# One attention visit for the second batch, casts on the DMA queue, and one more chunk of split products in the first tile of a fused attention and feed-forward kernel

## The chip, the core and the metric

The kernel runs on one core of a Trainium2 chip. The metric is the device time of one execution in microseconds (us). The profile is of one such execution and covers the five engines (PE for matrix products, ACT, DVE and POOL for elementwise work, SP for issuing transfers) and the core's 16 DMA engines.

## The reference

Linear attention over 8 batches (8 heads, 576 positions, head size 64), normalised per head, then a feed-forward layer over 4608 tokens of 512 features with 2048 hidden ones and a rational function between its two products:

```python
kv = np.einsum('bhsd,bhse->bhde', k, v)
out = np.einsum('bhsd,bhde->bhse', q, kv)
rms = np.sqrt(np.mean(out * out, axis=-1, keepdims=True) + 1e-06)
x = out / rms * g_norm            # to (tokens, 512)
h = x @ w_in
P = a[0] + a[1] * h + a[2] * h2 + a[3] * h3
Q = 1.0 + np.abs(b[0]) * np.abs(h) + np.abs(b[1]) * h2
return (P / (Q + 1e-06)) @ w_out
```

w_in and w_out come as 8-byte floats and are made into 4-byte ones on the chip.

## The kernel before

**Tiles and slots.** The tokens are cut into 9 tiles of 512: tile t holds the first 512 positions of batch t, and the ninth holds the last 64 positions of all batches. The hidden features are cut into 16 chunks of 128. One pair (tile, chunk) is a slot, and the loop at L784 writes the order of the instructions by hand (manual schedule): in slot i it issues the elementwise steps of h of chunk i (`ew_a` to `ew_d`, on ACT and DVE), the second product of slot i-2 (`gemm2`), the attention steps for the next tile that lists assign to the slot, the weight steps due in it, and the first product of slot i+1 (`gemm1`). Every engine works its own list in that order, so an instruction that waits holds all that stands behind it on its engine.

**Two kinds of products.** A "split" product takes both operands as a rounded high part and a low rest (type fp32r) and sums three matmuls (L531 to L533 for h, L599 to L601 for the output). An unsplit one is a single fp32 matmul, which the profile shows as two records (L527, L590). In tile 0, h of chunks 0 to `EARLY`-1 = 7 and all second products are unsplit.

**The front.** Before the loop, the k'v and the attention of batch 0 are done in a stage of their own. Its sums of squares (`first_ms`, L692), the reciprocal root (`first_newton`) and its spreading over 128 rows (`first_rb`, L708) work on blocks of `BW` = 64 columns, `NBLK` = 4 for each half tile.

**Attention of batch 1** is spread over tile 0 (`attention0`, L505). Each of four head pairs has a visit of its own: `att_kv1` (20 matmuls of 64 columns, L351, then two ACT copies into kvf, L270) in slots 1, 3, 5 and 7, and `att_o` (one fp32 matmul with q, L430, then a square and a copy on ACT, L438 and L439) in slots 2, 4, 6 and 8. All pairs share one PSUM buffer ("at") and one SBUF buffer for q ("qr"), so `att_o` fetches the next pair's q (`fetch_next_q`) only after its own matmul. It also fetches the next pair's k and v, and after the last pair the first of batch 2.

**Weights.** A unit is two chunks of w_in ("wi") or w_out ("wo"), 1 MiB as it comes. `schedule` (L141) holds for each unit the slot of its fetch (-1: before the loop), of its conversion (`signed` and `lowbits` on ACT, or `lowbits` on DVE for units in `ON_VECTOR`; `conv_b1`, `conv_add` on DVE) and of its split, and the rooms for its raw words, its fp32 form and its high and low parts.

**Split by transfer.** `split_w` casts the high part on ACT (L244). In the next slot POOL writes the negated high part (L250), and a POOL transfer adds the fp32 original to it in place (L251). `split_x0` does the same with x of tile 0, two head pairs at a time, its high part cast on ACT (L258) in slots 1 and 3.

**Queues.** All loads are issued by SP in program order, on one DMA queue (q1); transfers that cast or accumulate are issued by POOL (q0).

Of the kernel before, what the change touches and what calls it, by code (L numbers as in the profile page):

```python
# [23 lines left out]
def linear_attention_then_rational_ffn(  # L24
# [17 lines left out]
    P = 128  # L42
# [20 lines left out]
    NC = 7  # L63
    HW = TW // 2
    MAIN = 8 * P
    NBLK = 4
    BW = HW // NBLK
    kv0 = [wpool.tile([P, 2, MAIN], F32, tag=g, name=f"first_{g}") for g in ("g4", "g5")]
    qa0 = wpool.tile([P, NPAIR * HW + NC], F32, tag="g6", name="first_qa")
# [65 lines left out]
    def f32(t):  # L135
# [3 lines left out]


    schedule = {  # L141
# [16 lines left out]
    }  # L158
    units = list(schedule)

# [8 lines left out]
    for c in range(4, NF, 2):  # L169
        made[schedule["wi", c][1] + 1].append(("wi", c, None))  # L170

    EARLY = 8
    ON_VECTOR = (("wi", 6),)

    def unsplit(t, c):
        return t == 0
# [77 lines left out]
    def split_x0(g):  # L254
        pool, tag = ((xpool, "xA"), (wpool, "e"))[g]
        xt = pool.tile([P, 2, 2, TW], F32R, tag=tag, name=f"x_0_{g}")
        of = x0[:, 2 * g:2 * g + 2]
        ACT.copy(xt[:, :, 0], of)  # L258
        x.setdefault(0, []).extend((xt[:, p, 0], xt[:, p, 1]) for p in range(2))
        lows.append((xt[:, :, 1], xt[:, :, 0], of))  # L260

# [4 lines left out]
    def split_kv(t, pairs, ps):  # L266
        n = pairs.stop - pairs.start
        made = [ps[js, 0:n * D].rearrange("p (n d) -> p n d", n=n) for js in heads]
        for js, m in zip(heads, made):
            ACT.copy(kvf[js, pairs, js], m)  # L270
        if t == 1:
            return None
        for js, m in zip(heads, made):
            ACT.copy(kvh[js, pairs, js], m)

        def rest():
            for js in heads:
                DVE.tensor_tensor(kvl[js, pairs, js], kvf[js, pairs, js], f32(kvh[js, pairs, js]), ALU.subtract)
        return rest
# [28 lines left out]
    kvms, qrs, qs, sqs, rs, rbs, xf = {}, {}, {}, {}, {}, {}, {}  # L308

    def fetch_kv(t, p):  # L310
        tag, bufs = ("rb", 2) if p >= 2 and t > 1 else (f"kvm{p % 2}", 1)
        kvms[t, p] = work.tile([P, 2, 4, P], F32, tag=tag, name=f"kvm_{t}_{p}", bufs=bufs)
        nc.sync.dma_start(kvms[t, p], kv[t, p])

# [30 lines left out]
    def kv_products(t, ps, k, p):  # L345
        m = kvms.pop((t, p))
        ends = kvms[t][:, p // 2]
        for c in range(5):
            for js in heads:
                a, b = (m[:, 0, c], m[:, 1, c]) if c < 4 else (ends[:, 0], ends[:, 1 + p % 2])  # L350
                PE.matmul(ps[js, k * D:(k + 1) * D], a[:, js], b[:, js], start=(c == 0), stop=(c == 4))  # L351

    def att_kv1(t, p):
        ps = ps_at.tile([P, TW], F32, tag="at", name=f"kvp_{t}_{p}", bufs=1)
        kv_products(t, ps, 0, p)
        qs[t, p] = qrs.pop((t, p))
        split_kv(t, slice(p, p + 1), ps)

    def att_kv4(t, ps):
        if t >= NB:  # L360
            return None
# [2 lines left out]
        fetch_first_kv(t + 1)  # L364
        return lambda: split_kv(t, slice(0, NPAIR), ps)

    def att_kv_of_third(t, _):
        return att_kv4(t, ps_at.tile([P, TW], F32, tag="at", name=f"kvp_{t}", bufs=1))() if t == 2 else None

    x_rest = dram.tile([NPAIR, P, NB * R], F32, tag="x_rest", name="x_rest", bufs=1)  # L370

# [50 lines left out]
    def att_o(t, p):  # L422
        if t == LAST:
            sqs[t, p] = work.tile([P, TW], F32, tag="at", name=f"sq_{t}_{p}", bufs=4)
            ACT.activation(sqs[t, p], xf[t, p], AF.Square)
            return
        ps = ps_at.tile([P, TW], F32, tag="at", name=f"op_{t}_{p}", bufs=1)
        q = qs.pop((t, p))
        if t == 1:
            PE.matmul(ps, kvf[:, p], q, start=True, stop=True)  # L430
        else:
            qh, ql = q
            PE.matmul(ps, kvh[:, p], ql, start=True, stop=False)  # L433
            PE.matmul(ps, kvl[:, p], qh, start=False, stop=False)  # L434
            PE.matmul(ps, kvh[:, p], qh, start=False, stop=True)  # L435
        sq = work.tile([P, TW], F32, tag="at", name=f"sq_{t}_{p}", bufs=4)
        xf[t, p] = xpool.tile([P, TW], F32, tag=f"xf{p}", name=f"xf_{t}_{p}")
        ACT.activation(sq, ps, AF.Square)  # L438
        ACT.copy(xf[t, p], ps)  # L439
        sqs[t, p] = sq  # L440
        if t == 1:
            if p + 1 < NPAIR:
                fetch_kv(t, p + 1)
            else:
                fetch_first_kv(t + 1)
            fetch_next_q(t, p)

    def att_ms(t, _):
# [41 lines left out]
    attention = {s: [] for s in range(NF)}  # L490
    for p in range(NPAIR):
        if p == 0:
            attention[0].append((att_kv_of_third, 0))
        attention[2 * p].append((att_q, p))
        attention[2 * p + 1].append((att_o, p))
        attention[(11, 12, 13, 13)[p]].append((att_norm, p))
    attention[3].append((fetch_last_kv, 0))
    attention[8] += [(att_rest, 0), (att_ms, 0)]
    attention[9].append((att_rstd, 0))
    fillat = {att_norm: 1, att_kv_of_third: 1, att_rest: 1, att_q: 1, att_rstd: 2}  # L500
    attention[10] += [(att_rd, 0), (att_rb, 0), (att_rb, 1)]

    fillat0 = {}
    attention0 = {s: [] for s in range(NF)}
    for f, at in ((att_kv1, [1, 3, 5, 7]), (att_o, [2, 4, 6, 8]), (att_ms, [9]), (att_rstd, [9]), (att_rd, [10]), (att_rest_first, [10]), (fetch_last_kv, [11]), (att_rb, [11, 11]), (att_norm, [12, 12, 13, 13])):  # L505
        for p, k in enumerate(at):
            attention0[k].append((f, p))

# [224 lines left out]
            DVE.tensor_copy(x0[:, p, halves[0]], o0[p][0])  # L733
    for u in at_slot(0, -1)[:1]:
        fetch_w(u)
    fetch_kv(1, 0)
    fetch_ends(1)
    fetch_q(1, 0)
    for u in at_slot(0, -1)[1:]:
        fetch_w(u)  # L740
    ms0 = ps_at.tile([P, TW], F32, tag="ms", name="ms_0", bufs=1)
    first_ms(0)
    for p in range(NPAIR):
# [40 lines left out]
    for i, (t, c) in enumerate(slots[:-1]):  # L784
        q_made = ew_a(t, c, ph)
        for todo in lows:

            tc.add_manual_dep(low_by_transfer(*todo).ins, q_made.ins.name, beside, reason="negated beside h")
        lows.clear()
        if i:  # L790
            ew_d(*slots[i - 1])
        rest = {0: [], 1: [], 2: []}
        shifts = []
        convs = [lambda u=(k, n), j=j: conv_add(u, both if j is None else (one, two)[j]) for k, n, j in made.get(i, [])]

        ew_b(t, c, ph, convs[:1])
        if i == LAG:
            ph = gemm1(0, i + 1)
        if i >= LAG:
            gemm2(*slots[i - LAG])  # L800
            if slots[i - LAG][1] == NF - 1:
                evacuate(slots[i - LAG][0])
        for u in at_slot(2, i):
            split_w(u)
        if i in (1, 3):
            split_x0(i // 3)
        if i == 0:
            ph = h0[1]
        elif i in (1, 3):
            ph = gemm1(0, i + 1)  # L810
        if t + 1 < NTILE:
            for step, p in (attention0 if t == 0 else attention)[c]:
                todo_dve = step(t + 1, p)
                if todo_dve:
                    rest[fillat0.get(step, 2) if t == 0 else fillat[step]].append(todo_dve)
            for u in at_slot(0, i):
                fetch_w(u)
        for u in at_slot(1, i):
            signed(u)
            lowbits(u, both, "V" if u in ON_VECTOR else "S")  # L820
            shifts.append(u)
        rest[2] += convs[1:]
        if t == 0 and c == NF - 3:
            rest[2] += [split(1, p) for p in range(NPAIR // 2)]
        if t and c == NF - 2:
            ph = h_last
        elif 4 <= i < len(slots) - 2:
            ph = gemm1(*slots[i + 1])
            if 0 < t < NTILE - 1 and c == NF - 3:
                h_last = gemm1(t, NF - 1)  # L830
        if c == NF - 2 and t < NTILE - 1:
            xl = [split(t + 1, p) for p in range(NPAIR // 2 if t == 0 else 0, NPAIR)]
            if t == 0:
                rest[0] += xl
            for k in range(2 if t else 0):
                rest[k].append(xl[k])
                rest[2].append(xl[2 + k])
        if i == 0:
            rest[2].append(lambda: conv_add(u2, one))
        rest[2] += [lambda u=u: conv_b1(u, both) for u in shifts]  # L840
        ew_c(t, c, lambda k: [f() for f in rest[k]])
# [55 lines left out]
```

## Time and profile before

| | us |
|---|---|
| median of 3 runs | 879.95 (879.93 to 879.99) |
| profiled execution | 879.79 |
| its span, first to last instruction | 877.7 |
| PE busy | 870.7 (99%) |
| DVE busy | 757.7 (86%) |
| ACT busy | 687.5 (78%) |
| POOL busy | 73.3 (8%) |

The profiled execution takes 2.1 us beyond its span and lies 0.16 us under the median. In a timeline line the columns are: start, duration, engine, source line, operation, output and inputs, count and, in brackets, idle time of the engine before it with what ended it. Matmuls are pipelined, so that their records overlap; the distance from one start to the next is what a matmul costs. Tile 0 runs from about 24 us to 137 us.

### The profile page before, as it was taken

What the parts mean: (1) busy time and instruction counts of PE and PEld (TensorE: products, weight loads), DVE (VectorE), ACT (ScalarE), POOL (GpSimd) and SP (SyncE); (2) the same over time, 40 slices, a digit from 0 to 9 for tenths busy, and PEclk for the clock granted to TensorE, in tenths of its full rate; (3) what the DMA queues carried; (4) which work ended last, traced back from release to release, by engine and by line L of the source; (5) the groups of instructions that cost most, each with busy time, mean ns of one, the idle gap of its engine ahead of it and who ended that gap; (6) DMA issues with size and microseconds to landing.
All of it is one profiled execution on the core that took longest, in us unless ns stands there. A gap on an engine that the chain in (4) does not pass through costs nothing.

```text
span 877.7 us, 11994 instructions
## 1 busy us (share of the span) xinstructions
PE 870.7 (99%) x4468; PEld 683.9 (78%) x4468; DVE 757.7 (86%) x1185; ACT 687.5 (78%) x1142; POOL 73.3 (8%) x63
## 2 busy tenths in 40 slices
PE   9999999999999999999999999999999999999997
PEld 7545657888888888878888888888878887888886
DVE  4988998979987998879887998799879987998887
ACT  5999889877876788777877787768867786787665
POOL 2131435413000000000000000000000000000000
PEclk9999999999999999999999999999999999999999
DMA  9987638554122203040303111020102020201001
GB/s 364 406 262 226 145 73 216 138 127 97 60 73 90 50 6 115 30 122 1 119 19 104 31 61 72 25 50 17 69 12 50 13 84 1 49 1 49 1 0 49
DMA packets 32650, 76.27 MB, mean 87 GB/s; under 512 B 6032, under 2 KB 7568, under 8 KB 32592
## 3 DMA queue, kind: packets, MB, share of 16 engines
q1 hardware_dynamic: 29600, 65.81, 22.0%
q0 software_dynamic: 2848, 9.44, 5.9%
q8 instruction: 35, 0.57, 0.3%
q10 hardware_dynamic: 144, 0.26, 0.1%
q14 instruction: 23, 0.19, 0.1%
HBM read 55.45 MB, written 10.62 MB: 75 GB/s over the span
## 4 chain that ended last, share of the span: by engine, by line
PE 91%; DVE 5%; ACT 2%; issue 1%; DMA 1%; SPq 0%; ACTq 0%
PE h L531 14%; PE h L532 13%; PE h L533 13%; PE acc L599 12%; PE acc L601 12%; PE acc L600 12%; PE acc L590 5%; PE h L527 2%; PE kvp L351 2%; PE ms L451 1%; DMA first_g<-in_first_dram 1%; PE op L435 1%; PE op L433 1%; PE op L434 1%; DVE u L545 1%
## 5 line engine op out<-in xcount | busy, mean ns | idle before, releaser
L541 ACT ACTIVATE d<-h 128x512 f32<-128x512 f32 x143 | 85.6, 599 | 139.4 <-PE h L533 138.3
L543 DVE SCALAR_TENSOR_TENSOR q<-d,b1abs,q 128x512 f32<-128x512 f32 x143 | 107.2, 749 | 83.7 <-ACT q L542 83.5
L531 PE MATMUL h<-x,wihl 128*128 128x512 f32 (+1 forms) x420 | 166.2, 396 | 0.0
L532 PE MATMUL h<-x,wihl 128*128 128x512 f32 (+1 forms) x420 | 162.7, 387 | 0.0
L533 PE MATMUL h<-x,wihl 128*128 128x512 f32 (+1 forms) x420 | 162.6, 387 | 0.0
L599 PE MATMUL acc<-woh,gl 128*128 128x512 f32 x316 | 123.1, 389 | 0.1
L600 PE MATMUL acc<-wol,gh 128*128 128x512 f32 x316 | 122.9, 389 | 0.0
L601 PE MATMUL acc<-woh,gh 128*128 128x512 f32 x316 | 122.9, 389 | 0.0
L554 ACT ACTIVATE d<-q,bias 128x512 f32<-128x512 f32 x143 | 105.6, 738 | 13.9 <-DVE q L543 12.5
L544 ACT ACTIVATE u<-h,na 128x512 f32<-128x512 f32 x143 | 112.5, 787 | 0.0
L555 ACT ACTIVATE d<-d,bias 128x512 f32<-128x512 f32 x143 | 103.6, 725 | 4.7
L561 DVE SCALAR_TENSOR_TENSOR u<-u,na,d 128x512 f32<-128x512 f32 x143 | 106.7, 746 | 0.0
L551 DVE SCALAR_TENSOR_TENSOR u<-u,na,h 128x512 f32<-128x512 f32 x143 | 106.1, 742 | 0.6
L559 DVE SCALAR_TENSOR_TENSOR q<-q,d 128x512 f32<-128x512 f32 x143 | 98.4, 688 | 0.2 <-ACT d L555 0.2
L545 DVE TENSOR_TENSOR u<-u,h 128x512 f32<-128x512 f32 x143 | 98.0, 685 | 0.0
L542 ACT ACTIVATE q<-h,abg 128x512 f32<-128x512 f32 x143 | 97.9, 685 | 0.0
L531 PEld LDWEIGHTS h<-x,wihl 128*128 128x128 f32 x420 | 78.9, 188 | 24.0 <-issue 6.2
L532 PEld LDWEIGHTS h<-x,wihl 128*128 128x128 f32 x420 | 78.9, 188 | 17.0 <-issue 1.2
L533 PEld LDWEIGHTS h<-x,wihl 128*128 128x128 f32 x420 | 78.9, 188 | 16.2
L578 DVE TENSOR_TENSOR gl<-u,gh 128x512 fp32r<-128x512 f32 x127 | 90.8, 715 | 0.0
L567 DVE SCALAR_TENSOR_TENSOR u<-q,u 128x512 f32<-128x512 f32 x127 | 87.5, 689 | 2.5
L577 ACT CAST gh<-u 128x512 fp32r<-128x512 f32 x127 | 80.3, 632 | 3.5 <-DVE u L567 3.4
(170 smaller groups left out, 1403.0 us busy)
## 6 DMA issues: line engine op xcount, KB each, us to landing
kvm<-in_kv_dram SPq DMA_DIRECT2D x28, 512.0 KB
raw_wo<-in_w_out_dram SPq DMA_DIRECT2D x8, 1024.0 KB
out_dram<-ob SPq DMA_DIRECT2D x16, 512.0 KB
qr<-in_qT_dram SPq DMA_DIRECT2D x28, 256.0 KB
rb<-rd SPq DMA_DIRECT2D x28, 256.0 KB
raw_wi<-in_w_in_dram SPq DMA_DIRECT2D x6, 1024.0 KB
wihl<-wiw POOLq DMA_DIRECT2D x6, 512.0 KB, 4.7
kvt<-in_kv_rest_dram SPq DMA_DIRECT2D x7, 384.0 KB
```

The lines of the kernel that those rows point to most:

```text
L531: PE.matmul(ph, wh, xl, start=(kc == 0), stop=False)
L532: PE.matmul(ph, wl, xh, start=False, stop=False)
L533: PE.matmul(ph, wh, xh, start=False, stop=(kc == NPAIR - 1))
L543: q_made = DVE.scalar_tensor_tensor(q, d, b1abs, q, ALU.mult, ALU.add)
L544: ACT.activation(u, ph, AF.Identity, bias=na[:, 2:3], scale=na[:, 3:4])
L545: DVE.tensor_tensor(u, u, ph, ALU.mult)
L551: DVE.scalar_tensor_tensor(u, u, na[:, 1:2], ph, ALU.add, ALU.mult)
L554: ACT.activation(d, q, AF.Ln, bias=bias[:, 2:3], scale=QSC)
L561: DVE.scalar_tensor_tensor(u, u, na[:, 0:1], d, ALU.add, ALU.mult)
L599: PE.matmul(o, gl[:, ss], wh, start=(c == 0), stop=False)
L600: PE.matmul(o, gh[:, ss], wl, start=False, stop=False)
L601: PE.matmul(o, gh[:, ss], wh, start=False, stop=(c == NF - 1))
```

## The change

- `NBLK` goes from 4 to 2: the front's blocks have 128 columns.
- k'v of batch 1: the four `att_kv1` are replaced by one `att_kv` in slot 3 (80 matmuls, then two ACT copies for all pairs), `att_o` moves to slots 4, 5, 6 and 7, `att_rest_first` from slot 10 to slot 9. k and v of all four pairs and the first q are fetched before the loop, behind four weight units. The first k and v of batch 2 are fetched right behind the visit, in slot 3.
- x of tile 0: the high parts are cast by POOL transfers in slot 0, and the low parts follow one after the other, in slots 2 and 3 (before: 2 and 4).
- `EARLY` goes from 8 to 7: h of the eighth chunk is a split product. Unit ("wi", 6) is therefore split in slot 3 instead of 17, and its `lowbits` moves from DVE to ACT.
- The map of rooms is new; ("wi", 14) and ("wo", 10), ("wo", 12) and ("wo", 14) are fetched one or two slots later.

```diff
-    NBLK = 4
+    NBLK = 2
...
-        ("wi", 6): (-1, 1, 17, "g4", "f4", ("f10", "f12")),
+        ("wi", 6): (-1, 1, 3, "g4", "f4", "g4"),
...
-        ("wi", 14): (3, 8, 10, "g4", "f12", "g4"),
-        ("wo", 10): (4, 9, 23, "g5", "f13", ("f5", "f4")),
-        ("wo", 12): (6, 11, 25, "g7", "f14", ("f7", "f9")),
-        ("wo", 14): (8, 13, 27, "g1", "f15", ("f11", "f13")),
+        ("wi", 14): (4, 8, 10, "g5", "f12", "g5"),
+        ("wo", 10): (6, 9, 23, "g7", "f13", ("f3", "f5")),
+        ("wo", 12): (8, 11, 25, "g1", "f14", ("f7", "f9")),
+        ("wo", 14): (10, 13, 27, "g3", "f15", ("f11", "f13")),
...
-    EARLY = 8
-    ON_VECTOR = (("wi", 6),)
+    EARLY = 7
+    ON_VECTOR = ()
...
-        ACT.copy(xt[:, :, 0], of)
+        POOL.dma_start(xt[:, :, 0], of)
...
-        lows.append((xt[:, :, 1], xt[:, :, 0], of))
+        return xt[:, :, 1], xt[:, :, 0], of
...
-        tag, bufs = ("rb", 2) if p >= 2 and t > 1 else (f"kvm{p % 2}", 1)
+        tag, bufs = ("rb", 2) if p >= 2 else (f"kvm{p % 2}", 1)
...
-    def att_kv1(t, p):
-        ps = ps_at.tile([P, TW], F32, tag="at", name=f"kvp_{t}_{p}", bufs=1)
-        kv_products(t, ps, 0, p)
-        qs[t, p] = qrs.pop((t, p))
-        split_kv(t, slice(p, p + 1), ps)
...
-    def att_kv_of_third(t, _):
-        return att_kv4(t, ps_at.tile([P, TW], F32, tag="at", name=f"kvp_{t}", bufs=1))() if t == 2 else None
+    def att_kv(t, _):
+        if t <= 2:
+            return att_kv4(t, ps_at.tile([P, TW], F32, tag="at", name=f"kvp_{t}", bufs=1))()
...
         if t == 1:
-            if p + 1 < NPAIR:
-                fetch_kv(t, p + 1)
-            else:
-                fetch_first_kv(t + 1)
             fetch_next_q(t, p)
...
-    for f, at in ((att_kv1, [1, 3, 5, 7]), (att_o, [2, 4, 6, 8]), (att_ms, [9]), (att_rstd, [9]), (att_rd, [10]), (att_rest_first, [10]), (fetch_last_kv, [11]), (att_rb, [11, 11]), (att_norm, [12, 12, 13, 13])):
+    for f, at in ((att_kv, [3]), (att_o, [4, 5, 6, 7]), (att_rest_first, [9]), (att_ms, [9]), (att_rstd, [9]), (att_rd, [10]), (fetch_last_kv, [11]), (att_rb, [11, 11]), (att_norm, [12, 12, 13, 13])):
...
     for u in at_slot(0, -1)[:1]:
         fetch_w(u)
-    fetch_kv(1, 0)
-    fetch_ends(1)
-    fetch_q(1, 0)
     for u in at_slot(0, -1)[1:]:
         fetch_w(u)
+    fetch_first_kv(1)
+    fetch_last_kv(0, 0)
+    fetch_q(1, 0)
...
-        if i in (1, 3):
-            split_x0(i // 3)
+        if i == 0:
+            x0_lows = [split_x0(g) for g in range(2)]
+        if i in (1, 2):
+            lows.append(x0_lows[i // 2])
```

`att_kv4`, which the new `att_kv` calls, does the four pairs' products, then `fetch_first_kv(t + 1)` (two k and v of 512 KiB and the ends of 384 KiB), then the copies.

More of the change, by code (lines that the diff above doesn't have):

```diff
@@ L427, in att_o @@
         ps = ps_at.tile([P, TW], F32, tag="at", name=f"op_{t}_{p}", bufs=1)
-        q = qs.pop((t, p))
+        q = qrs.pop((t, p)) if t == 1 else qs.pop((t, p))
         if t == 1:
@@ L492, in linear_attention_then_rational_ffn @@
         if p == 0:
-            attention[0].append((att_kv_of_third, 0))
+            attention[0].append((att_kv, 0))
         attention[2 * p].append((att_q, p))
@@ L499, in linear_attention_then_rational_ffn @@
     attention[9].append((att_rstd, 0))
-    fillat = {att_norm: 1, att_kv_of_third: 1, att_rest: 1, att_q: 1, att_rstd: 2}
+    fillat = {att_norm: 1, att_kv: 1, att_rest: 1, att_q: 1, att_rstd: 2}
     attention[10] += [(att_rd, 0), (att_rb, 0), (att_rb, 1)]
```

10 rows, old and new, of the table schedule are left out of this document.

## The prediction

> **What bounds the kernel now.** I read the page first, then the waits of PE.
>
> ```profile
> PE 870.7 (99%) x4468; PEld 683.9 (78%) x4468; DVE 757.7 (86%) x1185; ACT 687.5 (78%) x1142; POOL 73.3 (8%) x63
> DMA  9987638554122203040303111020102020201001
> ```
>
> ```profile
> PE idle L645 <- POOL zero L82: 1.0, 1, 1.0
> PE h L527 <- DVE x L713: 0.4, 1, 0.4
> ```
>
> PE is busy from end to end, and the two longest of its waits are 1.0 and 0.4 us, both in the front. So a matmul taken away is worth its own distance to the next one, unless PE then waits for something. The second line shows what could come late: the DMA engines are full in the first two slices and a half, some 55 us. The stretches of tile 0 show it in numbers (columns: stretch, its length, busy time and count of PE, PEld, DVE, ACT, POOL; clock, DMA share, GB/s):
>
> ```profile
> 21.00:46.00 25.00, 25.00 (x105) 13.28 (x104) 23.68 (x37) 23.08 (x32) 4.18 (x2) 1.00 1.03 407
> 46.00:53.00 7.00, 6.89 (x17) 2.93 (x16) 6.39 (x11) 6.78 (x10) 0.00 (x0) 1.00 1.06 336
> ```
>
> Up to 46 us loads run at 407 GB/s with nothing left over. Here the chip moves data as fast as it can, and the order of the loads decides what is late. The change alters that order and adds transfers, so there are two sums: PE's own work, and the arrival of the loads.
>
> **PE's work.** The timeline of PE in tile 0 (starts and distances matter, not the durations):
>
> ```profile
> 28.80 0.69 PE L351 MATMUL kvp<-kvm 128*64 128x64 f32 x16
> ...
> 45.06 3.70 PE L590 MATMUL acc<-wow,g 128*128 128x512 f32 x8
> 48.87 1.13 PE L430 MATMUL op<-qr,kvf 128*128 128x512 f32 x2
> 49.83 3.60 PE L527 MATMUL h<-x,wiw 128*128 128x512 f32 x8
> 53.26 3.60 PE L590 MATMUL acc<-wow,g 128*128 128x512 f32 x8
> 56.79 0.69 PE L351 MATMUL kvp<-kvm 128*64 128x64 f32 x16
> ...
> 57.52 3.70 PE L527 MATMUL h<-x,wiw 128*128 128x512 f32 x8
> 61.06 3.60 PE L590 MATMUL acc<-wow,g 128*128 128x512 f32 x8
> 64.49 1.02 PE L430 MATMUL op<-qr,kvf 128*128 128x512 f32 x2
> 65.35 3.60 PE L527 MATMUL h<-x,wiw 128*128 128x512 f32 x8
> 68.78 3.60 PE L590 MATMUL acc<-wow,g 128*128 128x512 f32 x8
> ...
> 73.38 0.39 PE L532 MATMUL h<-x,wihl 128*128 128x512 f32 x1
> ...
> 75.67 0.39 PE L533 MATMUL h<-x,wihl 128*128 128x512 f32 x1
> ```
>
> ```profile
> 132.15 0.69 PE L351 MATMUL kvp<-kvm 128*64 128x64 f32 x16
> ...
> 134.64 0.50 PE L531 MATMUL h<-x,wihl 128*128 128x512 f32 x1
> ```
>
> An unsplit chunk costs 64.49 - 61.06 = 3.43 us, an attention product 65.35 - 64.49 = 0.86. A visit of k'v costs 57.52 - 56.79 = 0.73; the chunk ahead of it grows to 56.79 - 53.26 = 3.53 and the one behind to 61.06 - 57.52 = 3.54, so 0.94 in all, and four are 3.76. The one visit that exists, for batch 2, costs 134.64 - 132.15 = 2.49, with the same edges 2.70. **One visit: -1.06.** The rest products now stand beside the sums of squares, which saves about one more pair of edges: **-0.21**.
>
> Of a split chunk, the second matmul starts at 73.38 and the twelfth at 75.67: 0.229 each, 2.75 for twelve. Against 3.43, **the eighth chunk: -0.68**. Its low weights are made as x's second low part was before, beside slot 4:
>
> ```profile
> 56.23 1.24 POOL L251 DMA_DIRECT2D x<-x  x1 [0.31 <-POOL x L250]
> ```
>
> ```profile
> x<-x POOLq DMA_DIRECT2D x2, 512.0 KB, 7.9
> ```
>
> 56.23 + 7.9 = 64.1, and PE comes to this chunk at 65 or later; if not, it waits for what is missing.
>
> One wait goes: the second product took 48.87 - 45.06 = 3.81 us to reach where 3.54 is due, and 0.10 too long itself. It stood behind ACT's copies of kvf:
>
> ```profile
> 47.46 1.04 ACT L258 CAST x<-x 128x1024 fp32r<-128x1024 f32 x1
> 48.39 0.42 ACT L270 COPY kvf<-kvp 64x64 f32<-64x64 f32 x2
> ```
>
> ```profile
> L270 ACT COPY kvf<-kvp 64x256 f32<-64x256 f32 x12 | 4.4, 366 | 0.2 <-PE kvp L351 0.2
> ```
>
> But in the new slot 3 the cast of ("wi", 6) takes the place of x's cast, and the two copies take 0.73 instead of 0.42. ACT comes there some 0.15 earlier (x's cast of slot 1 is gone, `lowbits` comes in its place), so kvf is ready at about 49.0. PE arrives at 28.80 + four chunks (13.72) + the visit (2.70) + one chunk (3.43) + the front (0.15, below) = 48.8. So **the wait is the same within 0.1: -0.37 and +0.35**.
>
> Front: the block rows are
>
> ```profile
> L283 ACT ACTIVATE r<-ms,bias 128x512 f32<-128x512 f32 x8 | 5.4, 674 | 0.0
> L283 ACT ACTIVATE r<-ms,bias 128x64 f32<-128x64 f32 x2 | 0.7, 352 | 0.8 <-PE ms L692 0.8
> L288 DVE SCALAR_TENSOR_TENSOR r<-ms,r 128x512 f32<-128x512 f32 x8 | 5.5, 690 | 0.9 <-ACT r L285 0.9
> L288 DVE SCALAR_TENSOR_TENSOR r<-ms,r 128x64 f32<-128x64 f32 x2 | 0.4, 222 | 1.1 <-ACT r L285 1.1
> ```
>
> and 64 columns more cost 64 x (674 - 352) / 448 = 46 ns on ACT, 67 ns on DVE. Three ACT steps are on the way to the weights' conversion and so to the first h: +0.15. The spread matmuls are halved, 1.05 us to some 0.55, but the first ones are done before DVE comes to use them, and behind the second ones PE then waits for DVE's conversion of the second chunk. I take **+0.15**; the bounds are -0.5 (the whole halving is kept) and +0.3 (both halves are late).
>
> Sum without new waits: -1.06 - 0.21 - 0.68 - 0.02 + 0.15 = **-1.8 us**. ACT gets a square and a copy in slots 5 and 7 for the two small copies that leave. That is covered by g's lead, here in slot 5 (used by PE at 68.78):
>
> ```profile
> 63.79 0.69 DVE L567 SCALAR_TENSOR_TENSOR g<-q,u 128x512 f32<-128x512 f32 x1
> ```
>
> POOL has room for the low part in slot 3 instead of 4 (8% busy). The rest products' own transfer is issued a slot earlier, with nothing due behind it on SP, and the later weight fetches still have two slots or more until their conversion.
>
> **The arrival of q.** The loads are one queue, first in, first out:
>
> ```profile
> 8.92 0.39 SPq L191 DMA_DIRECT2D raw_wo<-in_w_out_dram  x1
> ```
>
> ```profile
> 20.66 1.16 ACT L206 ACTIVATE raw_wo<-raw_wo 128x1024 f32<-128x1024 f32 x1 [0.51 <-DMA raw_wo<-in_w_out_dram]
> ```
>
> A weight unit issued at 8.92 can be used at 20.66; the 12 us between are the queue. After the change q of the second pair is issued when the first product is done, at about 50, and these stand between that unit and it: nine weight units (9 MiB; four of them from ahead of the loop, then "wo" 4, "wi" 10, "wo" 6, "wi" 12, "wo" 8), k and v of four pairs (2 MiB) and of two pairs of batch 2 (1 MiB), two ends (0.75 MiB), the first q and itself (0.5 MiB). That is 13.25 MiB = 13.89 MB; at 407 GB/s it is 34.1 us, and q could be used at 20.66 + 34.1 = 54.8.
>
> POOL's transfers take their share of the same engines. The low part of x, 0.5 MiB, in the stretch from 46 to 53:
>
> ```profile
> q1 hardware_dynamic: 512, 1.81, 64.3%
> q0 software_dynamic: 272, 0.52, 41.1%
> ```
>
> 41.1% of 7 us is 2.9 us of all engines, and q1 moved 1.81 MB where 407 GB/s make 2.85: 2.6 us lost. Both low parts now fall ahead of q: +5.8. The two casts are new. Their price lies between that of 0.52 MB of loads (1.3 us) and that of an accumulation (2.9); nothing, or a gain, is excluded, as the engines have no free time there. A cast reads one source and writes, an accumulation reads two and writes, so I take two thirds of 2.9, an estimate: 1.9 each, +3.8. q can be used at 54.8 + 5.8 + 3.8 = **64.4** (63.2 to 66.4).
>
> PE wants it in slot 5: 28.80 + seven chunks (24.01) + the visit (2.70) + one product (0.86) + front and wait (0.5) = **56.9**. It stands in PE's list ahead of h of chunk 6, so PE idles **7.5 us** (6.3 to 9.5), and everything after it is that much later. On ACT the square of this product holds the conversion of ("wo", 6) and, behind it, the steps of chunk 6, which wait for PE anyway. The k and v of the one visit land in time (20.66 + 16.4 + 3.8 = 40.9 for the fourth, wanted at 42.7), and the third and fourth q find a short queue.
>
> **A cold PE.** The start shows what PE does after idling:
>
> ```profile
> 0.98 4.15 PE L645 MATMUL idle<-zero 128*128 128x128 f32 x18 [0.98 <-POOL zero L82]
> ...
> 9.71 1.97 PE L679 MATMUL op<-first_qa,kvf 128*128 128x256 f32 x8
> ```
>
> 18 records of 128 columns in 4.15 us are 0.23 each, 8 of 256 columns in 1.97 are 0.25: half the rate for about 4 us. After 7.5 us without work I expect the same, half of 4 us lost: **+1.9** (0 to 2.1).
>
> By the Trainium skill, "TensorE: Matmul & The Clock Gate", Part 1, PE falls to half its clock after some 3.4 us idle and needs about as long to come back; by it the loss would be 1.7 us, an estimate. The start agrees; that a pause in the middle does this is shown by no row here.
>
> Total: -1.8 + 7.5 + 1.9 = +7.6, on 879.79 gives 887.4; the median lies 0.16 above the profiled execution, so **887.5 us**.
>
> **The rivals.**
> - *q comes in time* (other side): the casts, the low parts or k and v of batch 2 don't hold the queue, and q is there by 56.9. Then 879.95 - 1.8 = 878.15, just at the edge of what can be told from no change. For it: one q alone is 0.26 MB, 0.6 us at 407 GB/s, and the first one was never waited for. Against it: even with free POOL transfers 54.8 leaves 2 us, and low parts take more. By the Trainium skill, "DMA: Bandwidth & Descriptors", section "Anatomy of one DMA", a transfer takes about 2.0 us plus its bytes at 436 GB/s; taken alone that is 2.6 us and would mean this case, but the unit at 8.92 took 12.
> - *A wait without cold clock*: 885.6.
> - *A short wait*: casts and low parts cost half of what I think, or the second low part comes behind q: q at 58 to 60, a wait of 1 to 3 us, 879.3 to 881.3.
>
> **Chances.** Wait with cold clock 0.57, without it 0.23, short wait 0.08, q in time 0.12. About 0.2% (1.8 us) can be told from no change. In time splits evenly between faster and same, and the short wait counts as same; so faster 0.06, same 0.14, slower 0.80. The range goes from the middle of the short wait, 880.5, to the dearest casts with a cold PE: 879.95 - 1.8 + 9.5 + 2.1 = 889.8; left out are in time and half of the short wait, 0.16, and a little above.
>
> **What would show it.** Right: a wait of PE of 6 to 9 us before L430 in slot 5, put down to the DMA of q; matmuls at twice their distance behind it; the DMA row full to beyond 60 us; one group of 80 records at L351 near 43 us; twelve records for chunk 7. Wrong: no such wait, or q landing soon after its issue; or PE waiting for the k'v visit or for the low part of ("wi", 6) instead.

## The result and the profile after

| | us |
|---|---|
| before, median | 879.94 |
| after, median of 4 runs | 887.9 (887.43 to 888.61) |
| ratio, 95% interval | 1.0091 (1.0074 to 1.0109) |
| profiled execution after, its span | 888.26, 886.5 |

The kernel became slower by 8 us; the forecast was 887.5. The page of the changed kernel, PE and DMA rows:

```profile
PE 871.0 (98%) x4408; PEld 684.5 (77%) x4408; DVE 756.9 (85%) x1184; ACT 685.5 (77%) x1135; POOL 74.6 (8%) x65
DMA  9994637644031403030112112010102020201001
```

PE's busy time is the same to 0.3 us, though 60 records fewer ran: a PE at half clock is busy for longer with the same work. The waits of PE name the place:

```profile
PE op L425 <- DMA qr<-in_qT_dram: 8.1, 1, 8.1
PE idle L636 <- POOL zero L82: 1.0, 1, 1.0
```

One wait that was not there before is eight times as long as the next. The timeline of PE around it (line numbers have moved: L425 is the attention product, L518 the unsplit h, L581 the second product):

```profile
43.02 0.69 PE L351 MATMUL kvp<-kvm 128*64 128x64 f32 x16
...
45.50 3.70 PE L581 MATMUL acc<-wow,g 128*128 128x512 f32 x8
49.07 1.10 PE L425 MATMUL op<-qr,kvf 128*128 128x512 f32 x2
50.00 3.60 PE L518 MATMUL h<-x,wiw 128*128 128x512 f32 x8
53.43 3.60 PE L581 MATMUL acc<-wow,g 128*128 128x512 f32 x8
65.12 2.05 PE L425 MATMUL op<-qr,kvf 128*128 128x512 f32 x2 [8.09 <-DMA qr<-in_qT_dram]
66.95 4.95 PE L518 MATMUL h<-x,wiw 128*128 128x512 f32 x8
71.75 3.60 PE L581 MATMUL acc<-wow,g 128*128 128x512 f32 x8
75.18 1.02 PE L425 MATMUL op<-qr,kvf 128*128 128x512 f32 x2
```

The one visit takes 45.50 - 43.02 = 2.48 us, and the first product comes 3.57 behind it, hardly later than the 3.54 that are due. Then PE waits until 65.12 for the second q. What follows is slow: 66.95 - 65.12 = 1.83 for a product that takes 0.86, and 4.80 for a chunk that takes 3.43. The stretches (behind POOL's busy time stand the granted clock, the share of full speed at which PE may run, then DMA share and GB/s):

```profile
53.00:60.00 7.00, 4.03 (x10) 1.52 (x8) 5.04 (x9) 6.81 (x11) 3.68 (x2) 0.96 1.06 329
60.00:66.00 6.00, 0.88 (x1) 0.50 (x2) 5.58 (x8) 1.87 (x3) 3.65 (x2) 0.50 1.06 314
66.00:72.00 6.00, 6.00 (x11) 2.57 (x10) 0.69 (x1) 3.19 (x5) 0.00 (x0) 0.69 0.52 126
```

While PE waits the DMA engines are full (1.06), and the clock stands at 0.50. In stretches of 0.1 us it falls at 59.44, 2.4 us after PE ran out of work at 57.03, and is back at 1.00 at 69.68. So PE works cold, at half clock, for 69.68 - 65.12 = 4.56 us, which costs half of that, 2.28. SP had issued that q long before:

```profile
43.75 0.92 SPq L313 DMA_DIRECT2D kvm<-in_kv_dram  x2
45.61 0.33 SPq L317 DMA_DIRECT2D kvt<-in_kv_rest_dram  x1
50.20 0.33 SPq L321 DMA_DIRECT2D qr<-in_qT_dram  x1
```

From its issue to its use pass 65.12 - 50.20 = 14.9 us for 256 KiB, with batch 2's k and v issued ahead of it. The formula of the Trainium skill ("DMA: Bandwidth & Descriptors", "Anatomy of one DMA") gives, as an estimate, 2.6 us for 256 KiB alone; it was fitted there to transfers that GpSimd issues, and SP issues this one. What the rest is, the experiments show.

### The profile page after: what moved, and what is told of

The parts are those of the page before. It is cut to its first block, busy times and chain, and to the rows that moved or that the text cites. A ratio compares the mean times of both kernels' runs of the same rounds, so it can differ in the third digit from the quotient of the medians.

```text
span 886.5 us, 11872 instructions
## 1 busy us (share of the span) xinstructions
PE 871.0 (98%) x4408; PEld 684.5 (77%) x4408; DVE 756.9 (85%) x1184; ACT 685.5 (77%) x1135; POOL 74.6 (8%) x65
## 4 chain that ended last, share of the span: by engine, by line
PE 96%; DMA 2%; ACT 1%; DVE 0%; SPq 0%; issue 0%; ACTq 0%
PE h L522 14%; PE h L523 14%; PE h L524 14%; PE acc L590 13%; PE acc L591 13%; PE acc L592 13%; PE acc L581 6%; PE h L518 2%; PE kvp L351 2%; DMA qr<-in_qT_dram 2%; PE ms L442 1%; DMA first_g<-in_first_dram 1%; PE op L429 1%; PE op L430 1%; PE op L428 1%; PE op L425 1%
## 5 line engine op out<-in xcount | busy, mean ns | idle before, releaser
L522 PE MATMUL h<-x,wihl 128*128 128x512 f32 (+1 forms) x360 | 143.4, 398 | 0.0
L523 PE MATMUL h<-x,wihl 128*128 128x512 f32 (+1 forms) x360 | 139.3, 387 | 0.0
L524 PE MATMUL h<-x,wihl 128*128 128x512 f32 (+1 forms) x360 | 139.3, 387 | 0.0
L590 PE MATMUL acc<-wohl,gl 128*128 128x512 f32 x256 | 99.6, 389 | 0.0
L591 PE MATMUL acc<-wohl,gh 128*128 128x512 f32 x256 | 99.6, 389 | 0.0
L592 PE MATMUL acc<-wohl,gh 128*128 128x512 f32 x256 | 99.6, 389 | 0.0
L590 PE MATMUL acc<-woh,gl 128*128 128x512 f32 x252 | 98.2, 390 | 0.0
L591 PE MATMUL acc<-wol,gh 128*128 128x512 f32 x252 | 98.1, 389 | 0.0
L592 PE MATMUL acc<-woh,gh 128*128 128x512 f32 x252 | 98.0, 389 | 0.0
L522 PEld LDWEIGHTS h<-x,wihl 128*128 128x128 f32 x360 | 67.6, 188 | 21.9 <-issue 5.1
```

The lines of the kernel that those rows point to most:

```text
L522: PE.matmul(ph, wh, xl, start=(kc == 0), stop=False)
L523: PE.matmul(ph, wl, xh, start=False, stop=False)
L524: PE.matmul(ph, wh, xh, start=False, stop=(kc == NPAIR - 1))
L590: PE.matmul(o, gl[:, ss], wh, start=(c == 0), stop=False)
L591: PE.matmul(o, gh[:, ss], wl, start=False, stop=False)
L592: PE.matmul(o, gh[:, ss], wh, start=False, stop=(c == NF - 1))
```

## The experiments

Theory: q is late because of what the queue and POOL's transfers put ahead of it, and a wait that long costs PE its clock besides. Rivals: q is late because its single buffer lets it be issued late; the casts alone make it late; what follows the wait is slow for another reason.

**Batch 2's k and v fetched after the last attention product, as before.**

```diff
-        fetch_first_kv(t + 1)
+        if t > 1:
+            fetch_first_kv(t + 1)
...
         if t == 1:
+            if p == NPAIR - 1:
+                fetch_first_kv(t + 1)
             fetch_next_q(t, p)
```

> Theory (queue): q of the second pair stands behind 13.25 MiB of loads. Here k, v and the ends of batch 2 (1.375 MiB, 3.5 us at 407 GB/s) are fetched after the last attention product, as in the kernel before, so PE's wait of 8.1 us becomes 4 to 5 us; with the cold clock behind it (2.3 us in the changed kernel) 882.0 to 884.5. Rival (late issue): q is late because its only buffer lets it be issued at 50 us, whatever is ahead; then 8 us of wait stay and the time is 887 to 889.

Measured: 880.06 us (1.0009, 1.0000 to 1.0019). The wait of PE:

```profile
PE op L426 <- DMA qr<-in_qT_dram: 2.0, 1, 2.0
```

The time is below the 882.0 that the theory allowed, and the wait half of what it expected. Late issue alone falls, as q is issued at the same time (50.29 against 50.20) and comes 6 us earlier. But 6 us is more than the 3.5 that were taken out. The DMA view of the changed kernel from 53 to 65 us, and of this one from 53 to 59, up to q's arrival:

```profile
q1 hardware_dynamic: 863, 2.81, 60.5%
q0 software_dynamic: 416, 1.05, 45.4%
```

```profile
q1 hardware_dynamic: 431, 1.37, 59.9%
q0 software_dynamic: 272, 0.52, 47.1%
```

q1 moved 1.44 MB more ahead of q after the change, just the 1.375 MiB that were taken out. q0 moved 1.05 MB, two transfers, and 0.52 MB, one, here. The second is the low part of ("wi", 6), issued by POOL at 56.45 and landed 8.6 us later in the changed kernel, at 65.05, just as q came; here it is issued at 56.51 and lands 7.5 later, at 64.0, behind q. Its share (45.4% of 12 us, less 47.1% of 6, is 2.6 us) and the 3.5 make the 6. The later a load lands, the more of the other queue's work gets in ahead of it, so the parts don't add up one by one.

**x's casts on ACT again.**

```diff
-        POOL.dma_start(xt[:, :, 0], of)
+        ACT.copy(xt[:, :, 0], of)
...
-        if i == 0:
-            x0_lows = [split_x0(g) for g in range(2)]
         if i in (1, 2):
-            lows.append(x0_lows[i // 2])
+            lows.append(split_x0(i - 1))
```

> The high parts of x are cast by ACT again (in slots 1 and 2, the low parts stay in slots 2 and 3). Theory: the two casts took 3.2 us of all DMA engines ahead of q, so q comes some 3 us earlier, the wait is 4.5 to 5.5 us, the cold clock stays, and the time is 884 to 885.5; ACT's extra 2 us make the wait for kvf longer by under 0.5 us. Rival (the casts alone make q late): no wait for q, about 879.

Measured: 880.86 us (1.0016, 1.0007 to 1.0025), in two groups: seven executions at 880.6 to 880.9 and three at 882.3 to 882.6. The waits of one of the three:

```profile
PE op L425 <- DMA qr<-in_qT_dram: 2.2, 1, 2.2
...
PE op L425 <- POOL x L250: 0.9, 1, 0.9
```

Both theories missed. The wait fell by 5.9 us: q comes 5.1 earlier, more than by the casts' own 3.2, for the reason above (here the low part of ("wi", 6) lands at 64.9, q at 59.99), and PE comes for it 0.8 later. The casts alone did not make q late either: 2.2 us are left. The second wait is the price on the other side, and twice the 0.5 that was allowed. The first attention product, at 49.86, now waits for kvf behind ACT's casts. The row names POOL, whose step ended at 49.53; ACT's copies of kvf, which the product reads, ended at 49.76.

**The wait filled with work.**

```diff
+        if t == 1 and p == 1:
+            filler = ps_at.tile([P, TW], F32, tag="ms", name="filler", bufs=1)
+            for _ in range(8):
+                PE.matmul(filler, kvf[:, 0], x0[:, 0], start=True, stop=True)
         ps = ps_at.tile([P, TW], F32, tag="at", name=f"op_{t}_{p}", bufs=1)
```

> Eight more fp32 products of 512 columns (6.9 us) are put ahead of the second attention product, into an unused PSUM bank; nobody reads them. The DMAs are the same. Theory (cold clock): PE waits 1.2 us instead of 8.1, up to the same moment, and the product and the chunk behind it are back at 0.9 and 3.4 us instead of 1.8 and 4.8: 885.3 to 886.0. Rival (no clock, something else slows what follows): 887.5 to 889.

Measured: 886.01 us (1.0070, 1.0057 to 1.0084), 1.9 below the changed kernel. PE after the filler, and the stretch:

```profile
65.06 1.10 PE L429 MATMUL op<-qr,kvf 128*128 128x512 f32 x2 [1.29 <-DMA qr<-in_qT_dram]
65.99 3.60 PE L522 MATMUL h<-x,wiw 128*128 128x512 f32 x8
69.43 1.02 PE L585 MATMUL acc<-wow,g 128*128 128x512 f32 x2
```

```profile
65.00:70.00 5.00, 4.94 (x12) 2.34 (x13) 1.29 (x2) 3.52 (x5) 0.00 (x0) 1.00 0.82 215
```

The wait ends at the same moment, the granted clock is 1.00, and the product and the chunk are back at 0.93 and 3.44. That the second part of the loss is the clock is shown.

**Six products instead of eight.** The edit is the same with `range(6)`.

> Six instead of eight extra products ahead of the second attention product: PE waits about 2.9 us. Theory 1 (the clock is judged over windows that run freely, so a wait of 2 to 3 us turns it cold in some executions: the run with a wait of 2.0 us had 880.0 in six and 881.7 to 881.9 in four of ten): two groups of times, about 886.0 and 887.7. Theory 2 (only a wait of more than some 3.4 us turns it cold): all at 886.0.

Measured: 885.99, 887.31, 887.44 and 888.82 us, median 887.38 (1.0085, 1.0071 to 1.0099). Three of four executions lost the clock; in the profiled one (888.82) PE waited 2.8 us. Theory 2 falls. Theory 1 holds in its mechanism, as will be seen, but has no place for 888.82. The kernel with the wait of 2.0 us (k and v late) gave 879.8 to 880.1 in six executions and 881.7 to 881.9 in four. The stretch behind the waits of 2.0 us and of 2.2 us (casts on ACT) in the two profiles:

```profile
60.00:64.00 4.00, 4.00 (x11) 1.77 (x10) 3.85 (x7) 3.82 (x6) 2.94 (x2) 1.00 0.75 184
```

```profile
60.00:64.00 4.00, 4.00 (x6) 1.77 (x7) 3.42 (x6) 3.81 (x7) 2.54 (x1) 0.59 0.93 232
```

One kept its clock, the other ran at 0.59 on average. The granted clock in the traces tells why. It was cold for 10.24 us in the changed kernel (from 59.44), 6.83 with six products (from 64.16) and 3.41 with the casts on ACT (from 60.72): three, two and one times 3.41. So the clock changes on a grid of 3.41 us, and what counts is how much of a wait lies in one step of it:

| profile | wait of PE, us | most of it in one step, us | clock after it |
|---|---|---|---|
| changed kernel | 8.1 | 2.40 in the step before the fall | half |
| casts on ACT | 2.2 | 2.17 | half |
| six products | 2.8 | 2.12 in the step before the fall | half |
| k and v late | 2.0 | 1.46 | full |
| rooms for q, k and v late, blocks of 64 (below) | 2.0 | 1.26 | full |
| eight products | 1.3 | 0.91 | full |

In the last three the clock falls only when the kernel's work is over, and the grid is counted back from there. By these six the limit lies between 1.46 and 2.12 us in one step. Where the grid falls differs from execution to execution, so a wait of some 2 us gives two groups of times. The clock came back only at the end of a step that PE had worked through. With six products PE worked cold from 64.85 to 70.98, which costs 3.1 us; one step less leaves 1.4. That fits 888.8 and 887.3 to 887.4 beside 886.0; it is an estimate for the executions without a profile.

The Trainium skill ("TensorE: Matmul & The Clock Gate", Part 1) names an idle window of some 3.4 us and says that its window runs freely. The length and the free run agree with the 3.41 us and the two groups of times. That the whole window must be idle does not: 2.1 us of it were enough here.

**Rooms for q.** The second and third q get rooms that tile 0 doesn't use and are fetched before the loop.

```diff
-        qrs[t, p] = work.tile([P, TW], F32, tag="qr", name=f"qr_{t}_{p}", bufs=1)
+        tag = ("qr", "qh", "ql", "qr")[p] if t == 1 else "qr"
+        qrs[t, p] = work.tile([P, TW], F32, tag=tag, name=f"qr_{t}_{p}", bufs=1)
...
-        if t == 1:
+        if t == 1 and p == 0:
+            fetch_q(t, NPAIR - 1)
+        if t == 1 and p == NPAIR - 1:
             fetch_next_q(t, p)
...
-    fetch_q(1, 0)
+    for p in range(3):
+        fetch_q(1, p)
```

> The q of the second and third pair get rooms of their own (those of qh and ql, idle in tile 0) and are fetched before the loop, behind the first q; the fourth is issued after the first product. Theory (queue): no wait for q at all, warm clock throughout, so what is left is PE's own saving: 877.9 to 878.8, 0.998 of before. Rival (something else comes late next: the low weights of the eighth chunk, or k and v for the one visit): 879.5 or more, with a PE wait of over 1 us at another line.

Measured: 877.65 us (0.9974, 0.9965 to 0.9984), beside 879.84 of before. PE:

```profile
53.44 3.60 PE L584 MATMUL acc<-wow,g 128*128 128x512 f32 x8
56.88 1.02 PE L426 MATMUL op<-qr,kvf 128*128 128x512 f32 x2
57.73 3.60 PE L521 MATMUL h<-x,wiw 128*128 128x512 f32 x8
61.17 3.60 PE L584 MATMUL acc<-wow,g 128*128 128x512 f32 x8
```

Up to 53.4 the two kernels run alike to 0.01 us. Then the product comes at 56.88 instead of 65.12 (8.24), and by the next second product, 61.17 instead of 71.75, the difference is 10.58: 8.24 of wait and 2.34 of clock. The spans differ by the same, 886.5 - 875.9 = 10.6. So the whole loss is this one place, and the rest of the change is a gain: 1.8 us of span (877.7 - 875.9), 2.2 by the medians. The difference lies outside the span. Every execution of before takes 2.1 us beyond it (2.05 to 2.17), those of the changed versions 1.8 (1.73 to 1.90, one 2.34); no run shows why. From the front's first product with q on (9.71 in before, 9.95 here) the gain is 2.0 us.

The edit moves only the issue of q, and the loads and transfers stay. So q was late by both: issued at 50 behind the single buffer, and behind all that the queues held by then.

**Parts of the gain**, each undone in the version with rooms for q. First the eighth chunk (`EARLY = 8`):

> The version with rooms for q, but the eighth chunk's h unsplit again (its weights are still split in slot 3). Prediction's term: a split chunk costs 2.75 us of PE, an unsplit one 3.43, so 877.65 + 0.68 = 878.3. Rival (the split chunk waits for its low parts, or its saving is lost to the change between product types): 877.5 to 877.8.

Measured: 878.21 us (0.9980, 0.9972 to 0.9989), 0.56 more where 0.68 was forecast. Then the front's blocks (`NBLK = 4`):

> The version with rooms for q, but the front in blocks of 64 columns again. Prediction's term: blocks of 128 cost 0.15 us (0.3 by the two traces' first chunks), so this is 877.3 to 877.5. Rival (the halved spread matmuls are a saving of 0.5): 878.1.

Measured: 878.14 us (0.9980, 0.9971 to 0.9989): the time of the rival, but not by its mechanism. The front, from its first product with q to the first second product of tile 0, with blocks of 128 (rooms for q) and of 64:

```profile
9.95 1.97 PE L673 MATMUL op<-first_qa,kvf 128*128 128x256 f32 x8
...
32.51 1.02 PE L584 MATMUL acc<-wow,g 128*128 128x512 f32 x2
```

```profile
9.65 1.97 PE L673 MATMUL op<-first_qa,kvf 128*128 128x256 f32 x8
...
32.08 1.45 PE L584 MATMUL acc<-wow,g 128*128 128x512 f32 x3
```

32.51 - 9.95 = 22.56 against 32.08 - 9.65 = 22.43: blocks of 128 cost 0.13 us, as forecast (0.15). The other 0.30 of the distance is the start, when the first loads came, which differs from execution to execution: it lies at 9.76 to 10.07 in the ten profiles with blocks of 128 and at 9.65 to 10.01 in the four with 64, while the front itself takes 22.54 to 22.57 in the ten and 22.42 or 22.43 in the three changed versions with 64. What makes the version slower comes at the ninth chunk:

```profile
PE h L526 <- DMA wihl<-wiw: 0.6, 1, 0.6
```

The low weights of the ninth chunk, sent by POOL at 63.31, land 9.6 us later, at 72.9, and PE came to this chunk at 71.6 and to them at 72.4. The version is 0.49 us ahead of rooms for q at 71.2 (71.17 against 71.66) and 0.32 behind at 75.6 (75.61 against 75.29). A small lead met the next late transfer. Then the casts (the edit shown above):

> The version with rooms for q, but x's high parts cast by ACT in slots 1 and 2. Theory: with q ahead of the queue the casts' share of the DMA engines costs nothing, and what they are worth is ACT's time ahead of the copies of kvf: PE waits about 0.9 us longer for the first attention product, 878.4 to 878.7. Rival (the casts are of no use): 877.6 or less.

Measured: 878.7 us (0.9987, 0.9978 to 0.9996), 1.05 more. The wait, and ACT's copies of kvf in this version and in rooms for q:

```profile
PE op L426 <- POOL x L250: 0.9, 1, 0.9
```

```profile
49.34 0.74 ACT L270 COPY kvf<-kvp 64x256 f32<-64x256 f32 x2
```

```profile
48.24 0.74 ACT L270 COPY kvf<-kvp 64x256 f32<-64x256 f32 x2
```

The copies come 1.10 us later, and the first attention product waits 0.9 us behind them (the row again names POOL, which ended 0.2 us before the copies). The casts' transfers cost nothing that shows once q is ahead of them: in rooms for q PE waits for no load in tile 0.

**Batch 2's k and v late, in the version with rooms,** with blocks of 128 and of 64.

> Rooms for q, and k and v of batch 2 fetched after the last attention product. Nothing waits for these loads in the version with rooms alone, so the theory (no wait for loads left) expects the same time, 877.5 to 877.8. Rival (the loads, moved to slot 7, now delay a low part or batch 2's attention): 878 or more.

> The same with the front in blocks of 64 columns. Theory: the front then saves 0.45 us (it did, up to slot 7, in the run before), and what it lost again to the low weights of the ninth chunk, which landed at 72.6 us behind batch 2's k and v, is not lost here, as the queue is short when they are sent: 877.1 to 877.3. Rival (the low weights are late by POOL's own time, whatever the queue holds): 877.9 to 878.2.

Measured: 878.82 (0.9988, 0.9979 to 0.9997) and 879.5 us (0.9999, 0.9990 to 1.0008). The theory fell in both. Two of the eleven executions of the second took 881.2 and 881.4, a group as after the other waits of 2 us. The wait and SP in the second one:

```profile
PE h L528 <- DMA wihl<-wiw: 2.0, 1, 2.0
```

```profile
62.32 0.37 SPq L191 DMA_DIRECT2D raw_wo<-in_w_out_dram  x1
62.73 0.94 SPq L313 DMA_DIRECT2D kvm<-in_kv_dram  x2
63.72 0.72 SPq L317 DMA_DIRECT2D kvt<-in_kv_rest_dram  x1
```

The fetch stands in slot 7, but with q in rooms of its own SP has nothing left to wait for and issues it at 62.7, right beside the low weights (sent at 63.47, landed 11.0 us later). Here a later place in the program held the fetch back only where SP had something to wait for.

**One weight unit held back instead:** ("wo", 10) fetched in slot 8, behind SP's wait for the last attention product; with blocks of 128 and of 64.

```diff
-        ("wo", 10): (6, 9, 23, "g7", "f13", ("f3", "f5")),
+        ("wo", 10): (8, 9, 23, "g7", "f13", ("f3", "f5")),
```

> Rooms for q, and unit (wo, 10) is fetched in slot 8 instead of 6, so that SP issues it behind its wait for the last attention product, at about 73 instead of 62.6 us. Nothing waited for loads in the version with rooms alone, so 877.5 to 877.8; with a shorter queue at 66 to 72 us the low weights of the ninth chunk land earlier than 71.9.

> The same with the front in blocks of 64 columns. Theory: PE is 0.45 us ahead from the front on, and the ninth chunk's low weights now land before PE wants them, at about 71.5, as one unit less stands in the queue beside them: 877.1 to 877.3. Rival (they are late by POOL's own time): 877.9 to 878.2 again.

Measured: 877.68 (0.9975, 0.9964 to 0.9985) and 877.48 us (0.9972, 0.9961 to 0.9983). The low weights land 7.6 and 7.4 us after their issue instead of 8.5 and 9.6, and no wait for them is left. The second is the best version found, 2.4 us under before. It misses the 877.1 to 877.3 expected: the 0.45 us expected of the blocks took the earlier start for their doing, and the 0.20 measured is near the front's 0.13. Its lead over the version with blocks of 128 is small against the spread of each (877.34 to 877.66 and 877.54 to 877.97).

## Why the prediction was right

- *The arrival of q.* Right in mechanism and place, and near in size: 64.4 was forecast, 65.1 came; the wait was 8.1 us against 7.5. But two errors in the sum partly cancelled. The casts took less than the two thirds of an accumulation that I took each: q0's share from 24 to 37 us is 24.5% of 13, 3.2 us for both instead of 3.8. And the low part of ("wi", 6), 2.6 us, was left out: I placed it only against its own chunk and not in q's way. With both put right the sum gives 66.4, so another 1.3 us stay unexplained, and that 64.4 came so near was in part luck.
- *The moment PE wants q.* 56.9 forecast, 57.0 measured.
- *The cold PE.* 1.9 forecast, 2.34 by the trace, 1.9 by the filled wait. That it was cold was argued from the start of the kernel alone; the granted clock of 0.50 and the filler show it.
- *PE's own work.* -1.8 forecast; in the version without the wait -1.8 by the span, -2.0 from the front's first product with q on, -2.2 by the medians, of which some 0.3 lie outside the span and in no term of the sum. The visit (2.48 against 2.49), the eighth chunk (0.56 in time against 0.68) and the front (0.13 against 0.15) hold singly. So do the rest products: from the second product ahead of them to the second one after it, PE takes 14.62 us (81.46 to 96.08) instead of 14.84 (82.96 to 97.80), 0.22 against 0.21.
- *The wait for kvf.* This term was mis-sized: 0.35 was forecast to stay, and 0.1 stayed (3.57 and 0.93 where 3.54 and 0.86 are due). ACT's copies in the changed kernel:

```profile
48.23 0.74 ACT L270 COPY kvf<-kvp 64x256 f32<-64x256 f32 x2
```

They end at 48.97, forecast 49.0, but in an execution that started 0.27 us later, at 9.98 against 9.71; PE came at 49.03. So ACT gained about 0.3 more than the 0.15 that I gave it.
- *The casts' use.* I gave them none, since they only seemed to shift ACT. They are worth 1.05 us, the wait for kvf that they avoid.
- *The rivals.* A wait without a cold clock is out for 8 us; a short wait is what two of the experiments made, in the changed kernel with k and v late or with the casts on ACT. q in time was out, and is what rooms for q make: 877.65, where 878.15 was worked out.

## What to carry to other kernels

Where the loads run at the chip's full rate, price every fetch by the bytes ahead of it in the queue, other queues' transfers included, and compare the moment it lands with the moment its reader wants it; here a small load behind a single buffer was the first to be late. A wait of some 2 us or more on PE can cost its length and, here, 1.4 to 2.8 us more at half clock. A wait of 2 us does so in some executions only, so look at all times of a kernel and not at its median alone. Moving a fetch down the program moves it in time only if its queue has something to wait for there.

## What the runs showed of the hardware

A transfer that casts fp32 to fp32r in rows of 2 KB on POOL's queue took 1.6 us of all 16 engines for 0.5 MiB, an accumulation of the same size 2.6 to 2.9, a plain load 1.3. Two queues share the engines so that a transfer issued later on the one can hold up an earlier one on the other: the same 256 KiB load took 14.9 us from issue to use, or 8.9 when 1.4 MB less stood ahead of it in its queue and one accumulation less got in from the other. And PE's clock changed on a grid of 3.41 us: it went to half after a step in which PE idled 2.1 us or more, kept full speed where 1.5 or less fell into one step, and came back after a step of work.
